# One attention and feed-forward kernel in another order, with its first weight loaded in 128-partition quarters

## The chip, the cores and the metric

The kernel runs on one core of a Trainium2 chip. Time is device time in microseconds (us) of one execution of the whole program; lower is better. Before the change three runs took 333.37, 333.5 and 333.9 us, median 333.5 us. The engines of the core have short names in the profile: PE is TensorE (matrix products), PEld its weight loads, DVE is VectorE, ACT is ScalarE, POOL is GpSimd and SP is SyncE. Each engine works through its own instructions strictly in order.

## The reference

Causal attention over 8 batches, 8 heads, 576 positions and 64 dimensions, with 16 "beacon" keys and values in front that every position may see, and then a two-layer feed-forward net with an ELU between its layers:

```
scores = q @ concat(beacon_k, k).T / sqrt(64), causal on the part of k
x = softmax(scores) @ concat(beacon_v, v)        -> 4608 tokens x 512
h = x @ w_in                                     -> 4608 x 2048
out = elu(h) @ w_out                             -> 4608 x 512, fp32
```

All inputs and the output are fp32 in DRAM; the kernel casts to 16 bits while loading.

## The kernel before

The program is one long list of small steps. `run(names)` at the end of the kernel takes words such as `F.4.6`, calls the step `F` with the arguments 4 and 6, and so issues its instructions to the engines' queues. Nothing reorders them: the place of a word in the list is its place in each queue that it uses, and waits on semaphores follow from the data and from the reuse of buffers. The words that matter here:

- `lq.b.n.h0.h1`, `lv.b.js`, `wi.c`, `wo.i`, `lk.b.n`: loads on POOL's DMA queue. `lq` brings q and k of a batch (0 to 2) straight into SBUF (L136); `lv` the values (L144, L149); `wi.c` a part of `w_in` (function `load_wi`, L161); `wo.i` a quarter of the rows of `w_out` (L165); `lk` copies q or k of a later batch (3 to 7) to a DRAM scratch in bf16 (L759). POOL's DMAs use eight semaphores in turn, so that each DMA is issued only when the eighth before it has landed.
- `lt.b.x`: two transposing DMAs from that scratch into SBUF, on SP's queue (L766), where the stores of the output stand too (`s`, L572, and those of `J`, L645).
- `T`, `cq`, `ck`, `cb`: for batches 0 to 2, transposes of q and k on PE (L265) and their copies out of PSUM (L278).
- `S.b.g`: a piece of 512 (batch 0: 416) columns of the scores of a batch on PE (L319); `x.b.g`: its exp on ACT (L334); `m`: the causal mask on DVE (L339). `S`, `L`, `W` and the `T` of batches 1 and 2 share two PSUM buffers of tag "S".
- `L`: sums of the exps on PE (L376, L418); `n`: their reciprocal, two ACT instructions (L433, L436); `W`: the product with the values on PE (L376); `M`: the scaled result into the feed-forward's input `xT` on DVE (L470 to L487). Parts `A` and `B` of batch 0 belong to tokens 0 to 255 and 256 to 575.
- `F.t.i`: 512 columns' worth of `h` for token tile t on PE (L510), into one of two PSUM buffers of tag "hps". Tiles 0 and 1 have 256 tokens, the other eight 512. `e` (exp, L520, ACT), `u` (relu, L526 on ACT or, with a `v` at the end, L528 on DVE) and `k` (L538, DVE) make the ELU from it. For the last two tiles part of `F` is done by a Strassen-like scheme: `X`, `H` (DVE), `P` (PE, L696), `K`, `E`, `U`, `V`.
- `G` (L559): the second product for tiles 0 and 1; `Q.t.a.b` (L626): for the others, in the Strassen-like form with `Z` and `wt` on DVE (L580) and `J` (L635 to L645) for what leaves PSUM. `o`, `s`: copy and store for tiles 0 and 1. `Jh` are the last two stores of the last tile.
- `warm` and `wm`: matmuls on zeros that keep PE busy while nothing has arrived. `tri`, `ident`: POOL makes the masks. `lp`: POOL pads keys of later batches (L775, L776).

`w_in` is held as 128 partitions x 4 (parts of the 512 rows) x 2048 columns in fp16. `load_wi(c)` has been called twice, for c = 0 and 1, each time with eight DMAs of 32 partitions x 2 parts x 1024 columns:

```
    def load_wi(c):
        f_ = slice(DF // 2 * c, DF // 2 * (c + 1))
        for g in range(2):
            for i in range(4):
                nc.gpsimd.dma_start(
                    out=w_in16[32 * i:32 * (i + 1), 2 * g:2 * g + 2, f_], in_=wi_v[i, :, g, :, f_])
```

`F.t.i` reads 128 columns of `w_in` per PSUM half for tiles of 512 tokens (i = 0 to 15) and 256 columns for tiles 0 and 1 (i = 0 to 7); it can start when the DMAs of those columns have landed.

## Time and profile before

| what | value |
|---|---|
| median of three runs | 333.5 us (333.37 to 333.9) |
| profiled execution: first to last instruction (span) | 331.3 us; the median lies 2.2 us above it |
| PE busy | 322.5 us, 97% of the span, 3576 matmuls |
| DVE busy | 291.8 us, 88% |
| ACT busy | 274.9 us, 83% |
| POOL busy | 88.3 us, 27% |
| granted TensorE clock | 0.998 of full speed |

A line of the timeline or of the chain has the start in us, the length in us, the engine, the source line, the operation and the tiles as output<-inputs, and at the end the idle time before it with what ended it. A line of a group has the number of instructions after an x, then the group's busy time in us and the mean length of one in ns. Instructions of one engine overlap a little, so a mean is longer than the step from one to the next. A line of waits has the total in us, the number of waits and the longest. A line of windows has the stretch, its length, and the busy time of PE, PEld, DVE, ACT and POOL with the instructions in brackets, then the clock, the DMA share and GB/s.

### The profile page before, as it was taken

Reading aid. Unit: us, or ns where it says so; the run is one execution under the profiler, and the core shown is the slowest. Engines: PE = TensorE matmul, PEld = TensorE weight load, DVE = VectorE, ACT = ScalarE, POOL = GpSimd, SP = SyncE. Lnnn points to the kernel's source line nnn. Section 1 sums busy time; section 2 is a strip of 40 time slices with the busy share of each in tenths; the row PEclk is TensorE's granted clock in tenths of the full one; section 3 lists DMA queues with packets and bytes.
Section 4 is the critical chain, followed back from the end, with each engine's and each line's share of the span. In section 5 each row is a group of like instructions: output and inputs, shape, how many; then the busy total and the mean of one; then the engine's idle time right before and its main releaser. Section 6 shows DMA issues by size and latency. Waiting matters only on the chain.

```text
span 331.3 us, 8764 instructions
## 1 busy us (share of the span) xinstructions
PE 322.5 (97%) x3576; PEld 208.3 (63%) x3576; DVE 291.8 (88%) x614; ACT 274.9 (83%) x446; POOL 88.3 (27%) x117
## 2 busy tenths in 40 slices
PE   8889999999999999999999999999999999999995
PEld 4657765544446565655665665556656788788784
DVE  3866888989998999999999789999999999999962
ACT  1898998699999998998898789996889687798730
POOL 8888266664008805000830050000000000000000
PEclk9999999999999999999999999999999999999999
DMA  9999999999989998952999098101100011011112
GB/s 114 172 169 182 199 191 172 160 148 156 164 193 69 172 164 135 97 117 60 104 192 153 3 110 133 33 0 34 66 32 3 33 65 34 32 65 34 64 66 95
DMA packets 129113, 34.66 MB, mean 105 GB/s; under 512 B 112944, under 2 KB 127536, under 8 KB 129072
## 3 DMA queue, kind: packets, MB, share of 16 engines
q0 software_dynamic: 94944, 18.49, 67.9%
q1 hardware_dynamic: 33408, 15.34, 20.8%
q8 instruction: 28, 0.46, 0.6%
q10 hardware_dynamic: 720, 0.26, 0.3%
q14 instruction: 13, 0.11, 0.1%
HBM read 37.22 MB, written 15.34 MB: 159 GB/s over the span
## 4 chain that ended last, share of the span: by engine, by line
PE 80%; DMA 10%; POOL 4%; ACT 2%; DVE 1%; issue 1%; DVEq 0%; POOLq 0%
PE hps L510 27%; PE ops L626 27%; DMA v<-in_v_dram 6%; PE sc L319 6%; PE ut L376 6%; PE hps L696 6%; PE ops L559 4%; DMA w_out<-in_moe_w_out_dram 3%; PE sx L626 2%; PE lt L376 1%; POOL qst L136 1%; POOL kst L136 1%; ACT et L334 1%; PE lt L418 1%; POOL v L149 1%
## 5 line engine op out<-in xcount | busy, mean ns | idle before, releaser
L510 PE MATMUL hps<-xT,w_in 128*128 128x512 f16 (+1 forms) x544 | 118.6, 355 | 0.3 <-DVE gt L550 0.2
L334 ACT ACTIVATE et<-sc 128x1024 f16<-128x1024 f32 (+2 forms) x114 | 103.6, 979 | 10.9 <-PE sc L319 10.8
L520 ACT ACTIVATE e<-hps 128x512 f32<-128x512 f32 x120 | 73.2, 617 | 18.9 <-PE hps L510 17.8
L626 PEld LDWEIGHTS <-gt 128*128 128x128 f16 x768 | 73.4, 98 | 19.9 <-issue 3.7
L538 DVE SCALAR_TENSOR_TENSOR gt<-e,r 128x512 f16<-128x512 f32 x112 | 75.4, 684 | 5.7 <-ACT r L526 5.0
L510 PEld LDWEIGHTS <-w_in 128*128 128x128 f16 x544 | 50.6, 98 | 41.9 <-issue 3.9
L526 ACT ACTIVATE r<-hps 128x512 f16<-128x512 f32 x88 | 54.3, 619 | 0.0
L626 PE MATMUL ops<-w_out,gt 128*128 128x256 f16 x368 | 48.0, 273 | 0.0
L626 PE MATMUL ops<-wt,gt 128*128 128x256 f16 x352 | 47.3, 273 | 0.0
L149 POOL DMA_DIRECT2D v<-in_v_dram x40 | 34.7, 914 | 10.6 <-DMA scr<-in_q_dram 3.6
L339 DVE TENSOR_TENSOR et<-et,triu 128x512 f16<-128x512 f16 (+4 forms) x108 | 31.6, 331 | 2.1 <-ACT et L334 2.1
L580 DVE TENSOR_TENSOR gt<-gt 128x1024 f16<-128x1024 f16 x48 | 32.2, 683 | 0.6 <-PE ops L626 0.3
L376 PEld LDWEIGHTS <-v 128*32 128x32 f16 (+1 forms) x800 | 17.4, 96 | 11.6 <-issue 4.2
L392 DVE TENSOR_TENSOR qk<-qk,et 128x672 f16<-128x672 f16 (+2 forms) x66 | 23.3, 367 | 0.5
L376 PE MATMUL ut<-et,v 128*32 128x464 f16 (+3 forms) x560 | 21.3, 296 | 0.0
L144 POOL DMA_DIRECT2D v<-in_beacon_v_dram x8 | 4.8, 595 | 61.8 <-PE lt L376 48.6
L528 DVE TENSOR_SCALAR r<-hps 128x512 f16<-128x512 f32 x24 | 16.4, 685 | 3.1 <-ACT e L520 2.8
L470 DVE TENSOR_TENSOR xT<-ut,rl 128x672 f16<-128x672 f32 (+12 forms) x26 | 16.4, 669 | 1.2 <-PE ut L376 0.7
L642 DVE TENSOR_TENSOR osb<-ops,sm 128x512 f32<-128x512 f32 x23 | 15.7, 682 | 1.0 <-PE ops L626 1.0
L559 PE MATMUL ops<-w_out,gt 128*128 128x512 f16 x64 | 16.4, 381 | 0.0
L735 DVE SCALAR_TENSOR_TENSOR gt<-e,r 128x512 f16<-128x512 f32 x24 | 15.9, 681 | 0.0
L706 ACT COPY kst<-hps 128x512 f32<-128x512 f32 x18 | 10.6, 588 | 5.9 <-PE hps L696 5.8
(113 smaller groups left out, 417.9 us busy)
## 6 DMA issues: line engine op xcount, KB each, us to landing
out_dram<-osb SPq DMA_DIRECT2D x35, 256.0 KB, 2.4
v<-in_v_dram POOLq DMA_DIRECT2D x24, 128.0 KB, 8.4
scr<-in_k_dram POOLq DMA_DIRECT2D x5, 576.0 KB, 12.8
scr<-in_q_dram POOLq DMA_DIRECT2D x5, 576.0 KB, 12.6
w_in<-in_moe_w_in_dram POOLq DMA_DIRECT2D x16, 128.0 KB, 5.5
w_out<-in_moe_w_out_dram POOLq DMA_DIRECT2D x4, 512.0 KB, 10.4
qst<-in_q_dram POOLq DMA_DIRECT2D x4, 288.0 KB, 9.4
kst<-in_k_dram POOLq DMA_DIRECT2D x4, 288.0 KB, 10.0
```

The lines of the kernel that those rows point to most:

```text
L149: nc.gpsimd.dma_start(out=vt[b][r0:r0 + n, j, :, :], in_=v[b, :, ilo[j]:ilo[j] + n, :].rearrange("h s d -> s h d"),)
L334: nc.scalar.activation(out=ets[b, d][:, :, a - EC2 * d:e - EC2 * d], in_=sc[b, g][:, :, a - c0:e - c0], func=AFT.Exp, bias=0.0, scale=SCALE)
L339: nc.vector.tensor_tensor(out=o, in0=o, in1=i, op=ALU.mult)
L376: nc.tensor.matmul(out=t[32 * i:32 * (i + 1), a - qa:e - qa], lhsT=ones[0:kc[j], :] if half is None else v16[0:kc[j], j, h, 32 * half:32 * ...
L392: (nc.vector if eng == "v" else nc.gpsimd).tensor_tensor(out=o, in0=t[0:rows, :, a:e] if n == 0 else o, in1=t[0:rows, :, col:col + e - a], ...
L510: nc.tensor.matmul(out=h[:, n_, :], lhsT=w_in16[:, cc, P * fc:P * (fc + 1)], rhs=xt[k][:, cc, a - TT * k:e - TT * k], start=(cc == 0), sto ...
L520: nc.scalar.activation(out=eb[t, i], in_=flat(hp[t, i]), func=AFT.Exp, bias=0.0, scale=1.0)
L526: nc.scalar.activation(out=rb[t, i], in_=flat(hp[t, i]), func=AFT.Relu, bias=0.0, scale=1.0)
L538: nc.vector.scalar_tensor_tensor(out=half(t, i), in0=eb[t, i], scalar=1.0, in1=rb[t, i], op0=ALU.subtract, op1=ALU.min)
L559: nc.tensor.matmul(out=ob[t, tb_], lhsT=gt[:, fc, P * tb_:P * (tb_ + 1)], rhs=w_out16[:, fc, :], start=(fc == 0), stop=(fc == NFC - 1))
L580: (nc.vector if eng == "v" else nc.gpsimd).tensor_tensor(out=o_, in0=a_, in1=b_, op=op_)
L626: nc.tensor.matmul(out=xy[t, n_][:, qd, :], lhsT=lw[:, P * qd:P * (qd + 1)], rhs=wt_[:, c, :], start=(first and c == 0 and (qd == 0 or (t, ...
```

## The change

Two functions and the list differ.

```diff
-    wi_v = moe_w_in.rearrange("(g i t d) f -> i d g t f", i=4, t=2, d=32)
+    wi_v = moe_w_in.rearrange("(g i t d) f -> g t i d f", i=4, t=2, d=32)
...
     def load_wi(c):
-        f_ = slice(DF // 2 * c, DF // 2 * (c + 1))
-        for g in range(2):
-            for i in range(4):
-                nc.gpsimd.dma_start(
-                    out=w_in16[32 * i:32 * (i + 1), 2 * g:2 * g + 2, f_], in_=wi_v[i, :, g, :, f_])
+        f_ = slice(DF // 4 * c, DF // 4 * (c + 1))
+        for cc in range(NCC):
+            nc.gpsimd.dma_start(out=w_in16[:, cc, f_], in_=wi_v[cc // 2, cc % 2, :, :, f_])
...
     def P_(t, g, ph):
-        if ph == 0:
+        if (t, g, 0) not in hx:
```

`w_in` still comes in 16 DMAs with the same bytes each, but a DMA now fills 128 partitions of one part and 512 columns, and `wi.0` to `wi.3` are four steps of four DMAs, one for each quarter of the columns, that stand apart in the list. The test in `P_` lets its phases come in another order.

The list has the same words as before, except that `wi.0` and `wi.1` have become `wi.0` to `wi.3`; all 1503 others are there once each, most of them at another place. The start and the places that the prediction names:

```diff
-    warm.4 lq.0.0.0.4 warm.4 lq.0.1.0.4 warm.4 wm.4 ident wm.4 T.0.0.0 bt wm.4 bk wm.4 wm.4
-    T.0.1.0 cb.0.0 cq.0.0.0 S.0.0.0 x.0.0.0 T.0.1.1 lq.0.0.4.8 cq.0.1.0 cb.0.1 S.0.1.0 x.0.1.0
...
-    M.0.A.1 x.1.2 S.1.1 x.1.1 W.0.A.0 M.0.A.0 S.0.3.3 x.0.3.3 S.0.2.2 wi.0 F.0.2 x.0.2.2 S.1.5
...
-    x.2.3 L.1.0 n.1.0 wt.1.0 G.0.1.2 H.1.2 M.1.0.0 W.1.0 u.1.0.v M.1.0.1 L.1.1 k.1.0 e.0.7 F.1.6
-    m.2.0.0 n.1.1 M.1.1.0 cb.2.3 W.1.1 M.1.1.1 e.1.6 u.0.7 u.1.6.v k.1.6 S.2.2 x.2.2 G.0.0.2
...
-    Q.9.77.84 Q.9.84.91 J.9.4 Q.9.91.98 J.9.5 Q.9.98.105 Jh.9.0 Q.9.105.112 Jh.9.1
+    warm.4 warm.4 wm.4 wm.4 wm.4 lq.0.0.0.4 lq.0.1.0.4 ident T.0.1.0 lq.0.0.4.8 bt cq.0.1.0 bk
+    warm.4 T.0.0.0 cb.0.1 cb.0.0 cq.0.0.0 S.0.1.0 T.0.1.1 S.0.0.0 x.0.1.0 x.0.0.0 T.0.0.1
...
+    x.0.0.2 m.0.0.2 S.0.2.3 x.0.2.3 L.0.A lv.0.0.1 n.0.A T.1.0.0 wi.0 T.1.1.0 W.0.A.1 cq.1.0.0
+    wm.4 lv.0.3.4 m.0.2.3 ck.1.1.0 S.0.3.2 x.0.3.2 M.0.A.1 W.0.A.0 wi.1 S.0.3.3 m.0.2.2 M.0.A.0
+    x.0.3.3 S.0.2.1 F.0.1 cb.1.2 S.0.3.1 cb.1.3 m.0.0.3 m.0.3.2 x.0.2.1 m.0.3.3 e.0.1 lq.1.0.4.8
+    S.1.4 x.0.3.1 wo.0 x.1.4 m.0.1.2 H.1.0 F.0.0 e.0.0 u.0.0 L.0.B W.0.B.1 k.0.0 wi.3 n.0.B
+    u.0.1.v F.0.2 e.0.2 u.0.2 M.0.B.1 W.0.B.0 M.0.B.0 S.1.3 x.1.3 F.0.3 S.1.5 e.0.3 k.0.1
...
+    e.1.4 m.1.0.1 H.2.2 ck.2.0.0 k.0.7 m.1.1.0 u.1.4.v x.2.4 L.1.1 L.1.0 lp.3.1 n.1.1 F.1.6
+    cb.2.0 M.1.1.0 k.1.4 n.1.0 M.1.0.0 lv.1.2.3.4 W.1.1 wo.2 W.1.0 M.1.1.1 S.2.7 wo.3 lk.3.1
...
+    k.2.14 x.3.1 Z.2.3.0 wt.4.0 k.2.3 Q.2.0.7 s.1.1 F.3.3 o.1.0 x.3.12 e.3.3 D.3.1.1 S.3.2
...
+    Q.2.14.21 D.3.1.2 Z.2.1.1 lk.4.0 lt.4.0 S.4.2 S.4.1 x.4.1 Q.2.21.28 k.3.3 D.3.1.3 J.2.0
...
+    F.4.10 e.4.10 u.4.10 e.4.14 Q.3.42.49 J.3.2 x.5.7 Q.3.56.63 F.4.6 F.4.12 D.4.3.3 u.4.6 e.4.6
...
+    Q.9.63.70 Z.9.4.0 Q.9.70.77 J.9.3 Q.9.77.84 Q.9.84.91 J.9.4 Q.9.91.98 J.9.5 Q.9.98.105 J.8.6
+    Q.9.105.112 Jh.9.0 Jh.9.1
```

## The prediction

> **What bounds the kernel now.** I read the first part of the page, then the stretches, then the groups of ACT, the waits, the chain and single places of the timeline.

> ```profile
> span 331.3 us, 8764 instructions
> PE 322.5 (97%) x3576; PEld 208.3 (63%) x3576; DVE 291.8 (88%) x614; ACT 274.9 (83%) x446; POOL 88.3 (27%) x117
> PE 80%; DMA 10%; POOL 4%; ACT 2%; DVE 1%; issue 1%; DVEq 0%; POOLq 0%
> 8.80:60.20 51.40, 48.58 (x906) 33.30 (x909) 40.15 (x95) 46.48 (x65) 35.40 (x51) 1.00 1.53 180
> 60.20:150.85 90.65, 90.65 (x899) 48.83 (x892) 85.27 (x182) 83.67 (x133) 31.27 (x34) 1.00 1.59 144
> 9.20:151.25 142.05, 139.23 (x1797) 82.17 (x1796) 125.42 (x276) 130.56 (x197) 66.28 (x83) 1.00 1.57 157
> 151.25:331.30 180.05, 175.66 (x1724) 122.20 (x1721) 162.94 (x329) 143.09 (x249) 14.13 (x17) 1.00 0.36 62
> ```

> PE is the bound: from 60.20 to 150.85 it is busy in 90.65 of 90.65 us, and it heads the chain with 80%. Since the change adds no matmul, the time can only grow by new holes in PE's work and shrink by filling old ones, which lie in the first 60 us and at the end. But ACT is close behind, with 130.56 of 142.05 us (91.9%) from its first exp to 151.25. The new list moves work between engines' queues, so the second engine is what I count.

> **The change, part by part.** *The loads.*

> ```profile
> L161 POOL DMA_DIRECT2D w_in<-in_moe_w_in_dram x8: 532/535/571, 13.1 to 19.5; - x8
> L165 POOL DMA_DIRECT2D w_out<-in_moe_w_out_dram x2: 762/764/765, 28.7 to 29.4; - x2
> 12.26 6.96 DMA v<-in_v_dram
> 29.40 10.87 DMA w_out<-in_moe_w_out_dram
> 23.89 0.69 DVE L480 TENSOR_TENSOR xT<-ua,rl 128x512 f16<-128x512 f32 x1 [0.32 <-PE ua L376]
> 24.70 1.05 PE L510 MATMUL hps<-xT,w_in 128*128 128x256 f16 x8
> ```

> Sixteen DMAs of 128 KB stay. One takes POOL 0.535 us to issue; the nearest 128-partition form is the `w_out` row's 0.764, so the new ones cost POOL between 0 and 16 × 0.23 = 3.7 us more. I take 0: the chain shows POOL waiting for landings (6.96 and 10.87 us), which covers it; without that cover `wi.3` would be issued up to 3.7 us late, against the 4 to 9 us by which, in my walk through the new list, loads land ahead of their first reader. How fast they land is bounded by rows too: the values before them land at 12.26 + 6.96 = 19.22, the last of the old eight at 24.37 (issued 19.5, landing row below), 0.64 us per 128 KB; `w_out` in 128 partitions landed 512 KB in 37.3 to 40.3, 2.9 us or 0.73 per 128 KB. So a quarter is there at 19.22 + 4 × 0.64 = 21.8 to 19.22 + 4 × 0.73 = 22.1. I take 21.8, the price of the same DMA size.

> ```profile
> DMA to landing us min/median/max: 4.9/5.6/6.4
> DMA to landing us min/median/max: 8.7/9.8/10.9
> ```

> Before, the first `F` at 24.70 had two conditions 0.2 us apart: the weights at 24.37 and `xT`, finished at 23.89 + 0.69 = 24.58. After, `F.0.1` stands behind `M.0.A.0`, and my walk has it near 22.5, about 2 us earlier.

> *The first stage.* That lead isn't kept. (The walk takes the new list word by word, each word's instructions at the lengths that the trace before has for them, each waiting for the words that it reads and for the buffers that it takes.) In it `F.0.2` waits about 1.3 us for a PSUM bank of tag hps, because `u.0.1.v` stands on DVE behind `k.0.0`; and `L.1.1 L.1.0 W.1.1 W.1.0` hold both S buffers, so that after `x.2.4` no scores can be made and ACT stands some 1.6 us. The end of `W.1.0` comes out at 60.2, and PE's matmuls behind it sum to what was left before at 60.20 too. So the start is worth 0 here (bounds: −2.2, the lead kept, and +2).

> *The stage to `F.4.6`.* At the word `F.4.6` PE has the same work left as before at 150.85, so that place measures the gain. `F.4.6` needs the bank that `u.4.10` frees, and behind ACT's part of that stand these in the list: 81 exps of scores, 57 exps and 38 relus of `F`, 18 instructions of reciprocals, 4 copies of keys, 3 of `J`. Before, up to 151.25:

> ```profile
> L334 ACT ACTIVATE et<-sc 128x1024 f16<-128x1024 f32 (+2 forms) x77 | 69.2, 974 | 9.2 <-PE sc L319 9.2
> L520 ACT ACTIVATE e<-hps 128x512 f32<-128x512 f32 x59 | 36.3, 621 | 6.3 <-PE hps L510 5.5 <-ACT sm L635 0.5 <-ACT hi L278 0.2
> L526 ACT ACTIVATE r<-hps 128x512 f16<-128x512 f32 x37 | 23.0, 624 | 0.0
> L436 ACT ACTIVATE rl<-rl 128x576 f32<-128x576 f32 (+2 forms) x8 | 5.5, 684 | 0.3
> L433 ACT ACTIVATE rl<-lt 128x576 f32<-128x576 f32 (+1 forms) x7 | 4.9, 693 | 1.9 <-PE lt L376 1.9
> L278 ACT COPY qk<-tp 128x1152 bf16<-128x1152 bf16 x3 | 3.3, 1112 | 0.8 <-PE tp L265 0.8
> L635 ACT COPY sm<-ops 128x512 f32<-128x512 f32 x4 | 2.4, 591 | 0.1
> L278 ACT COPY hi<-tp 128x1152 bf16<-128x1152 bf16 x1 | 1.2, 1180 | 0.0
> L433 ACT ACTIVATE rl<-la 128x512 f32<-128x512 f32 x1 | 0.7, 695 | 0.0
> L334 ACT ACTIVATE et<-sc 128x1024 f16<-128x1024 f32 x84 | 84.2, 1052 | 3.2 <-PE sc L319 3.1
> 9.20 1.62 ACT L334 ACTIVATE et<-sc 128x832 f16<-128x832 f32 x2 [7.12 <-PE sc L319]
> ```

> (The last but one is the full-size exps of the whole run.) The difference is 4 exps of scores more, 2 of `F` fewer, a relu and 2 reciprocal instructions more, a `J` copy fewer: +4 × 1.052 − 2 × 0.621 + 0.624 + 2 × 0.684 − 0.591 = +4.4 us. ACT's instructions overlap: these groups of the stretch (the first nine rows) sum to 146.5 us where 130.56 are busy, a factor of 0.89, so +3.9. ACT thus has 130.6 + 3.9 = 134.5 us to do by `F.4.6`, from about 8.8 on (before from 9.20). When it gets through depends on how densely it works, and the rows give 91.9% (whole stretch), 95.7% and 97.6%:

> ```profile
> 140.00:160.00 20.00, 20.00 (x238) 11.72 (x236) 19.10 (x44) 19.14 (x31) 1.04 (x2) 1.00 0.36 75
> 20.00:30.00 10.00, 9.28 (x218) 6.67 (x215) 5.67 (x15) 9.76 (x14) 8.57 (x15) 1.00 1.17 166
> ```

> By 91.9% `F.4.6` comes at 8.8 + 134.5 / 0.919 = 155.2; by 95.7% at 149.3; by 97.6% at 146.6. I take two stages. Up to 60.2 ACT did 46.48 us before. Ahead of `W.1.0` the new list has 31 exps of scores against 33, 14 of `F` against 15 and 6 relus against 5:

> ```profile
> L334 ACT ACTIVATE et<-sc 128x832 f16<-128x832 f32 (+2 forms) x33 | 28.2, 941 | 7.7 <-PE sc L319 7.7
> L520 ACT ACTIVATE e<-hps 128x512 f32<-128x512 f32 x15 | 9.1, 609 | 1.5 <-PE hps L510 1.2 <-ACT hi L278 0.2
> L526 ACT ACTIVATE r<-hps 128x512 f16<-128x512 f32 x5 | 3.0, 607 | 0.0
> ```

> That is −2 × 0.941 − 0.609 + 0.607 = −1.9, of which I let 0.7 be filled by words from behind (bounds 0 and 1.9): 45.3, or 88%. The remaining 134.5 − 45.3 = 89.2 I put at 95.7%, the value where ACT and PE both ran full, since ACT now is what PE waits for: 93.2 us. `F.4.6` then starts at 60.2 + 93.2 = 153.4, 2.55 us later than 150.85. That is 93.0% over all. The density at which nothing changes is 134.5 / (150.85 − 8.8) = 94.7%, or 94.4% with the tail below.

> Behind `F.4.6` ACT has 3.9 us less to do than before in 180.05 us with 143.09 busy, and PE with 175.66 busy bounds again; I count 0 there (±1).

> *The store queue.* SP works in order. The new list puts `lt.4.0` (the transposes of batch 4's keys and queries) directly behind `s.1.1`, a store that waits for `o.1.1` near 94, and `S.4.2` needs them at 100 to 103. The two prices of a transpose from issue to landing:

> ```profile
> L766 SPq DMA_TRANSPOSE kst<-scr x2: 2630/3445/4260, 70.0 to 72.7; - x2
> DMA to landing us min/median/max: 8.7/9.5/11.4
> L766 SPq DMA_TRANSPOSE kst<-scr x2: 1291/1612/1934, 87.0 to 91.5; - x2
> DMA to landing us min/median/max: 3.3/3.8/5.5
> ```

> (First pair from 60 to 83 us, while POOL's queue was full; second from 86 to 100, while it was quieter.) Landing lies between 94 + 3.3 = 97 (no stall) and about 94 + 11.4 = 105 (up to 5 us of PE). I take the quiet price, as the stretch is the nearest, hence 0 in the sum; the other end is a rival. `s.0.0` and `s.1.0`, moved later, hold two of three output buffers while `J.2.4` to `J.2.6` need them; stores land in 2.4 us against about 3.5 between `J`s, so 0 (bounds 0 to 3).

> ```profile
> out_dram<-osb SPq DMA_DIRECT2D x35, 256.0 KB, 2.4
> ```

> *The tail.* PE's last product waits for the copy of `Jh.9.0`:

> ```profile
> 326.34 0.37 ACT L746 COPY osb<-sx 128x256 f32<-128x256 f32 x1 [3.89 <-PE sx L626]
> 326.76 0.92 PE L626 MATMUL sx<-wt,gt 128*128 128x256 f16 x7 [0.46 <-ACT osb L746]
> ```

> With `Q.9.105.112` ahead of `Jh.9.0` that 0.46 goes: −0.5 (bounds −0.5 and 0, if `J.8.6`, now between, takes its place). `tri`, one place later on POOL, and `P`'s test cost nothing: POOL there waits for landings, and the test runs on the host.

> *The sum.* The profiled execution took 331.3 us of span and about 2.2 around it, equal to the 333.5 us median: 333.5 + 0 (start) + 2.55 (`F.4.6` later) + 0 (store queue) − 0.5 (tail) = 335.5.

> [...] The row: the old 32-partition loads landed at 0.64 us per 128 KB and the 128-partition `w_out` at 0.73. [...]

> **The rivals.**

> *The other side: ACT stays dense.* The new order feeds ACT so that it works at 95.7% from its first exp on, not only behind 60 us. For it: 97.6% between 20 and 30 us in the old list, where weights had just come. Against it: the exps of the first 60 us waited 7.7 us for scores (row above). `F.4.6` at 149.3, −1.55, and −0.5: 331.4. It ends faster from 94.4% on. At 97.6% it would be 333.5 − 4.25 − 0.5 = 328.8, the lowest I can construct.

> *Late transposes.* `lt.4.0` at the busy price: PE stands at `S.4.2`, ACT has no scores of batch 4 either, +3 (middle of 0 to 5 rounded up) on top of the forecast: 338.5, at most 340.5. For it: POOL's queue still carries `lk.4.0` just ahead of it. Against it: before, the transposes at 87 to 96 were quick.

> *The start was held by the load.* A quarter in place of a half is what matters, and the 2.6 us from 24.70 to 22.1 are kept through the first stage, ACT keeping pace: 333.5 + 2.55 − 2.6 − 0.5 = 332.9. For it: the first `F` follows the last landing by 0.3 us. Against it: `xT` was 0.12 us ahead of that `F`, so the load alone gave nothing.

> *Nothing changes.* The later `F.4.6` is only PE work in another order, PE finds filler, and the holes add to what the tail gives: 333.5.

> **How the numbers follow.** Forecast 0.38; late transposes 0.18; dense ACT 0.24; the load 0.10; nothing 0.10. The forecast is 335.5, its own range 334.2 (94.0% dense) to 337.5 (91.9%, rounded down for the part past 60 us). 0.2%, 0.67 us, is about what a measurement here can tell. Faster: dense ACT 0.24 and the load at 332.9 mostly, 0.08, with 0.02 of "nothing": 0.34. Same: 0.10, from "nothing" and the lower edge of the forecast. Slower: the rest, 0.56. The range goes from 328.8, the lowest of dense ACT, to 340.5, the highest of late transposes.

> **What would show it.** In the trace after: first `F` near 22.5, its weights landed by 22.1; the end of `W.1.0` near 60.2; ACT 88% busy up to there and near 95% from there; `F.4.6` near 153.4, with PE's waits there put down to relus or exps of ACT; `lt.4.0` landed before `S.4.2`; no wait of PE for `osb` in the last 2 us. Wrong would make me: an end of `W.1.0` more than 1 us from 60.2 (the first stage), PE standing for `kst` near 100 us (the queue), or a PE that stays without holes to 150 (ACT not bounding).

## The result, and the profile after

The changed kernel takes 346.7 us (median of four runs, 345.2 to 350.8) against 333.7: a ratio of 1.036, 95% interval 1.031 to 1.042. That is 12 to 13 us slower and above the 340.5 us at which my range ended. A ratio, here and below, leaves out a run that is more than 1.5% above the fastest of its kernel (here the one of 350.84 us). The profiled execution took 345.23 us, with a span of 343.5.

The first parts of the page of the kernel after (the rows of PE, PEclk and DMA show, in 40 slices of 8.6 us, the busy share of PE, the granted clock and the busy share of the DMA engines, in tenths), and its stretches, with the last two rows for the kernel before:

```profile
span 343.5 us, 8750 instructions
PE 325.3 (95%) x3576; PEld 209.8 (61%) x3576; DVE 290.5 (85%) x614; ACT 276.6 (81%) x446; POOL 92.3 (27%) x117
PE   6979999995999999889999999999999999999995
PEclk9998999999899999989999999999999999999999
DMA  9999999999999441999597090610110011020113
PE 79%; DMA 9%; ACT 4%; POOL 3%; DVE 2%; issue 2%; SPq 1%; DVEq 0%; POOLq 0%
```

```profile
8.80:60.20 51.40, 48.77 (x916) 33.48 (x916) 37.81 (x95) 46.31 (x65) 37.73 (x54) 0.97 1.47 168
60.20:150.85 90.65, 81.76 (x806) 42.37 (x798) 75.92 (x158) 75.78 (x116) 36.80 (x35) 0.97 1.59 137
164.35:343.50 179.15, 175.07 (x1684) 122.81 (x1681) 161.59 (x325) 140.33 (x244) 10.14 (x14) 1.00 0.29 58
8.80:164.35 155.55, 144.03 (x1859) 84.05 (x1855) 125.84 (x280) 135.03 (x202) 74.53 (x88) 0.97 1.54 149
8.80:150.85 142.05, 139.23 (x1799) 82.14 (x1800) 125.42 (x276) 130.16 (x197) 66.67 (x83) 1.00 1.57 157
150.85:331.30 180.45, 176.06 (x1728) 122.56 (x1725) 163.34 (x329) 143.49 (x250) 14.13 (x17) 1.00 0.36 63
```

Where PE had no hole before, from 60.20 to 150.85, it now lacks 8.9 us of 90.65, and the clock of this stretch is 0.97. `F.4.6` begins at 164.35, 13.5 us later than the 150.85 of before, and PE has about the same work left there (175.07 us busy against 176.06). Behind it the new order is 1.3 us quicker (179.15 us against 180.45), most of it this 1.0 us. So the loss is complete by `F.4.6`. The rows from 8.80 us to `F.4.6` divide it: PE was idle there for 155.55 − 144.03 = 11.5 us against 2.8 before, 8.7 more, and busy for 144.03 us against 139.23, 4.8 more; together 13.5. The idle part first. The longest waits of PE behind the first 8.8 us, and where they stand in its timeline:

```profile
PE sc L317 <- DMA qst<-scr: 4.2, 2, 3.5
PE hps L508 <- DVE r L526: 3.1, 1, 3.1
PE sc L317 <- issue: 2.1, 2, 1.9
PE sc L317 <- DMA kst<-scr: 1.4, 1, 1.4
```

```profile
23.66 0.38 PE L317 MATMUL sc<-hi 64*128 64x80 bf16 x5 [1.86 <-issue]
23.98 1.05 PE L508 MATMUL hps<-xT,w_in 128*128 128x256 f16 x8
...
78.87 0.39 PE L317 MATMUL sc<-kst 64*128 64x272 bf16 x4 [1.38 <-DMA kst<-scr]
...
86.46 0.40 PE L317 MATMUL sc<-qst 64*128 64x48 bf16 x6 [3.47 <-DMA qst<-scr]
...
109.71 0.63 PE L317 MATMUL sc<-qst 64*128 64x16 bf16 x10 [0.73 <-DMA qst<-scr]
...
147.54 1.20 PE L508 MATMUL hps<-xT,w_in 128*128 128x512 f16 x4 [3.09 <-DVE r L526]
```

There are five holes of over 0.3 us, 10.5 us together. None of them is put down to ACT. In order: `S.0.3.3`, which waits for nothing that the profile names; `S.3.8` and `S.3.3`, for the transposes of batch 3; `S.4.2`, for those of batch 4; and `F.4.1`, for a relu on DVE.

The busy part is the clock. Stretches after three of these holes, in the windows of the kernel after:

```profile
26.00:27.00 1.00, 1.00 (x7) 0.64 (x6) 0.96 (x6) 1.00 (x3) 0.51 (x1) 0.50 0.94 74
88.50:90.00 1.50, 1.50 (x5) 0.42 (x3) 0.15 (x1) 1.08 (x2) 0.93 (x1) 0.50 2.47 158
150.00:152.00 2.00, 2.00 (x14) 0.97 (x13) 2.00 (x5) 1.18 (x2) 0.00 (x0) 0.58 1.89 215
```

By the clock records of the trace the grant falls to 0.50 three times, for 3.4 us each, at 25.4, 86.8 and 148.3 us, 0.3 to 1.7 us behind the end of the holes of 1.86, 3.47 and 3.09 us. Each costs half of 3.4, so some 1.7 us, 5.1 in all, in which PE counts as busy. That is an estimate, and it roughly fits the 4.8 us by which PE was busy longer.

The last hole has its cause on DVE and SP:

```profile
146.20 0.69 DVE L638 COPY osb<-ops 128x512 f32<-128x512 f32 x1 [3.52 <-DMA out_dram<-osb]
```

`J.2.6` (L638) waits for an output buffer. `o.0.0` and `o.1.0` have filled two of the three and their stores stand far behind in the new list, so `J.2.4`, `J.2.5` and `J.2.6` share one; the store of `J.2.5` was issued at 139.73 and landed at 146.11. `u.4.9.v`, next on DVE, is what `F.4.1` needs.

### The profile page after: what moved, and what is told of

It is laid out like the page before. It is cut to its first block, busy times and chain, and to the rows that moved or that the text cites. A ratio compares the mean times of both kernels' runs of the same rounds, so it can differ in the third digit from the quotient of the medians.

```text
span 343.5 us, 8750 instructions
## 1 busy us (share of the span) xinstructions
PE 325.3 (95%) x3576; PEld 209.8 (61%) x3576; DVE 290.5 (85%) x614; ACT 276.6 (81%) x446; POOL 92.3 (27%) x117
## 4 chain that ended last, share of the span: by engine, by line
PE 79%; DMA 9%; ACT 4%; POOL 3%; DVE 2%; issue 2%; SPq 1%; DVEq 0%; POOLq 0%
PE hps L508 27%; PE ops L624 24%; PE sc L317 7%; PE hps L694 5%; PE ut L374 5%; DMA qst<-scr 5%; PE ops L557 4%; DMA v<-in_v_dram 2%; PE sx L624 2%; DMA out_dram<-osb 2%; PE lt L374 2%; ACT et L332 1%; PE tp L263 1%; POOL qst L136 1%; POOL kst L136 1%
## 5 line engine op out<-in xcount | busy, mean ns | idle before, releaser
L332 ACT ACTIVATE et<-sc 128x1024 f16<-128x1024 f32 (+2 forms) x114 | 104.6, 967 | 23.6 <-PE sc L317 23.5
L508 PE MATMUL hps<-xT,w_in 128*128 128x512 f16 (+1 forms) x544 | 120.4, 359 | 3.1 <-DVE r L526 3.1
L624 PEld LDWEIGHTS <-gt 128*128 128x128 f16 x768 | 74.6, 98 | 19.3 <-issue 2.0
L518 ACT ACTIVATE e<-hps 128x512 f32<-128x512 f32 x120 | 71.8, 613 | 10.1 <-PE hps L508 9.8
L524 ACT ACTIVATE r<-hps 128x512 f16<-128x512 f32 x88 | 52.7, 611 | 5.4 <-PE hps L508 4.5
L624 PE MATMUL ops<-w_out,gt 128*128 128x256 f16 x368 | 49.1, 277 | 0.0
L624 PE MATMUL ops<-wt,gt 128*128 128x256 f16 x352 | 46.5, 273 | 0.0
L149 POOL DMA_DIRECT2D v<-in_v_dram x40 | 35.6, 1036 | 6.8 <-issue 4.4
L526 DVE TENSOR_SCALAR r<-hps 128x512 f16<-128x512 f32 x24 | 16.4, 685 | 11.1 <-ACT e L518 11.1
L144 POOL DMA_DIRECT2D v<-in_beacon_v_dram x8 | 5.9, 738 | 43.1 <-PE lt L374 22.1
L317 PE MATMUL sc<-qst 64*128 64x80 bf16 (+13 forms) x160 | 12.4, 258 | 4.2 <-DMA qst<-scr 4.2
## 6 DMA issues: line engine op xcount, KB each, us to landing
out_dram<-osb SPq DMA_DIRECT2D x35, 256.0 KB, 2.4
```

What stands on the lines that cost most here:

```text
L149: nc.gpsimd.dma_start(out=vt[b][r0:r0 + n, j, :, :], in_=v[b, :, ilo[j]:ilo[j] + n, :].rearrange("h s d -> s h d"),)
L317: nc.tensor.matmul(out=s[:, h, a - c0:e - c0], lhsT=t[D * h:D * (h + 1), 1, P * j:P * (j + 1)], rhs=t[D * h:D * (h + 1), 0, NB + qa + a - ...
L332: nc.scalar.activation(out=ets[b, d][:, :, a - EC2 * d:e - EC2 * d], in_=sc[b, g][:, :, a - c0:e - c0], func=AFT.Exp, bias=0.0, scale=SCALE)
L508: nc.tensor.matmul(out=h[:, n_, :], lhsT=w_in16[:, cc, P * fc:P * (fc + 1)], rhs=xt[k][:, cc, a - TT * k:e - TT * k], start=(cc == 0), sto ...
L518: nc.scalar.activation(out=eb[t, i], in_=flat(hp[t, i]), func=AFT.Exp, bias=0.0, scale=1.0)
L524: nc.scalar.activation(out=rb[t, i], in_=flat(hp[t, i]), func=AFT.Relu, bias=0.0, scale=1.0)
```

## The experiments

Theories that the runs tell apart: **L**, the shape of the loads makes the DMA queue slower, so that everything behind is late; **O**, the new order does it by itself, by its queues (held buffers, transposes) or, as I had forecast, by asking too much of ACT; **F**, the hole near 22 us is a late instruction fetch.

**The loads alone, in the order before.**

```diff
-wi.0 F.0.2 ...   wi.1 F.0.4        (8 loads each: 32 partitions x 2 parts x 1024 columns)
+wi.0 wi.1 F.0.2 ...   wi.2 wi.3 F.0.4        (load_wi as after)
```

> The order before, with only w_in loaded in the new way (each half as two quarters, at the old places). Theory L (the load shape): a quarter load in 128 partitions makes 128 packets of 1024 B and some 384 of 4 B where the old one makes 64 of 2048 B, which in the traces is 283 us of DMA engine time for all of w_in against 190, or +5.8 us on 16 saturated engines. What is behind it on POOL's queue lands about 3.6 us later, and with it the scratch of batch 3 and its transposes, which batch 3's first scores need: PE stands 1 to 4 us near 82, with half clock behind it, 336 to 339 us. Theory O (the order alone is at fault): 333.7 us, no hole.

338.3 us against 334.5, ratio 1.012 (1.008 to 1.017). Theory O alone is out, as this order is the one of before; L's size came out, but not its place. The holes, in PE's timeline of this kernel:

```profile
37.62 0.45 PE L263 MATMUL tp<-identb,qst 96*64 96x96 bf16 x12 [1.83 <-DMA qst<-in_q_dram]
39.39 0.45 PE L263 MATMUL tp<-identb,kst 96*64 96x96 bf16 x12 [1.32 <-DMA kst<-in_k_dram]
```

It is not batch 3's transposes but the direct loads `lq.1.0.4.8` of batch 1, the next behind `w_in` on POOL's queue, that come late. Windows of the same kernel (its 20 to 30 and 30 to 40 us) beside the second of the kernel before, whose first stands in the prediction with 166 GB/s:

```profile
20.00:30.00 10.00, 8.74 (x184) 5.95 (x182) 4.98 (x14) 9.11 (x13) 7.62 (x11) 1.00 1.27 134
30.00:40.00 10.00, 6.85 (x160) 4.92 (x146) 6.32 (x12) 6.43 (x11) 6.13 (x10) 0.99 1.21 174
```

```profile
30.00:40.00 10.00, 9.88 (x173) 7.18 (x162) 8.99 (x16) 8.61 (x14) 4.97 (x8) 1.00 1.24 195
```

The queue moves 134 and 174 GB/s where it moved 166 and 195, with its engines as busy (the DMA share is 1.27 and 1.21 against 1.17 and 1.24). By the packet records the old loads are 1024 packets of 2048 B at 185 ns; the new ones are 1024 B at 106 ns, twice as many, and 6144 packets of 4 B besides.

**The old loads in the order after** (halves, at the places of `wi.0` and `wi.3`).

> The order after, with w_in loaded in the old way (32 partitions, halves, at the places of the first and the second quarter to be called). Theory L: the lag of the queue goes, batch 3's transposes land 3 to 4 us earlier, so of the holes 1.38 and 3.47 us and the half clock behind them (1.7 us) 4 to 5.5 us go; the hole of 1.86 us near 22 may go too, if it is a late instruction fetch in a full queue: 338 to 343 us. Theory O: 346 us, holes as they are.

345.0 us (341.6 to 346.3), ratio 1.031 (1.025 to 1.037). Four holes of over 2 us are there; the waits of PE:

```profile
PE sc L319 <- DMA qst<-scr: 5.0, 2, 2.6
PE hps L510 <- DVE r L528: 3.1, 1, 3.1
PE hps L510 <- DMA w_in<-in_moe_w_in_dram: 2.1, 1, 2.1
```

Batch 3's holes fall from 4.85 to 2.4 us, but batch 4's grows from 0.73 to 2.6: PE came to `S.4.2` 4.4 us earlier (at 104.6 in place of 109.0), and the transpose that it reads landed only 2.5 us earlier (107.2 in place of 109.7). A first half of `w_in` that lands later than the first quarter did takes another 2.1. So L explains only a part, and a hole that is taken away shows the next. The time itself is not clearly below the changed kernel's: the two intervals, 1.025 to 1.037 and 1.031 to 1.042, overlap. The span and mean clock of this execution have a second lesson, that with four holes of 2.1 to 3.2 us the clock stayed whole:

```profile
core 0: 339.9 us, clock 0.997
```

**The stores early, in the order after.**

```diff
-... F.6.4 s.0.0 D.6.2.2      ... k.4.9 s.1.0 Q.3.14.21
+o.0.0 s.0.0 M.2.0.0 ...      lt.4.1 s.1.0 F.3.12
```

> The order after, with the stores s.0.0 and s.1.0 put where their data is ready (behind o.0.0 and behind lt.4.1), so that only one of the three output buffers is in use for long. If the 3.09 us hole near 144 comes from the two held buffers, it goes, and with it the half clock behind it (1.6 us): 341.5 to 342.5 us. If it comes from a slow store alone, a hole of 1 us or more stays: 344 to 346 us.

344.1 us, ratio 1.031 (1.027 to 1.036). The hole near 144 is gone altogether, so the held buffers were its cause. Of the 4.7 us expected 2.6 came, by medians whose intervals overlap: at `S.4.2` there is now the wait

```profile
112.37 0.63 PE L317 MATMUL sc<-qst 64*128 64x16 bf16 x10 [2.86 <-DMA qst<-scr]
```

**The loads in 128 partitions, but in halves of 1024 columns.**

> The order after, w_in in 128 partitions but 1024 columns to a load (8 loads, two halves). By packet size (Theory L): 1024 packets of 2048 B as in the old loads and half as many of 4 B, some +2 us of queue in place of +5.8: the transposes of batch 3 come 2 to 3 us earlier than after the change, 340 to 344 us. If the span of partitions and not the packets sets the landing (32 partitions slower or faster than 128), it differs from the old loads in the new order by more than 2 us.

345.5 us, ratio 1.030 (1.025 to 1.036), no different from the old loads in this order. By the rule of the expectation that speaks against the span of partitions, but in this order the time doesn't tell the forms of the load apart (346.7, 345.0 and 345.5 us); the packet records do. The packets are of 2048 B again, and yet, in the packet records, they take 249 ns each in place of 185. By 40 us the queue has moved 5.66 MB, against 5.58 after, 6.07 with the old loads in this order and 6.29 before. So the packet's size isn't what costs: by the packet records a load that spans 128 partitions with one part of the rows costs more than the old form with either size of packet. Why, no run here shows.

**Batch 4's transposes ahead of the store**, on top of the early stores.

```diff
-Q.2.0.7 s.1.1 ... lk.4.0 lt.4.0 S.4.2
+Q.2.0.7 lk.4.0 lt.4.0 s.1.1 ... S.4.2
```

> As the run with early stores, and the transposes lt.4.0 put ahead of s.1.1 on SP's queue (lk.4.0 keeps its place on POOL's queue). If lt.4.0 was late because it stood behind a store that waited for DVE, it is issued near 93 instead of 102 and the hole at S.4.2 (2.86 us in the run with early stores, 0.73 in the new order itself) goes, with or without a half clock behind it: 339.5 to 341.5 us. If the transfers themselves are late, the hole stays: 344 us.

339.8 us, ratio 1.018 (1.014 to 1.022): 4.3 us less than the run before it, and no hole of PE over 0.25 us is left behind 88 us. The transfers are no quicker (issue to landing 9.9 us in the median between 85 and 115 us, against 5.4 in the run with early stores), only begun 8.5 us sooner: first issued at 94.2 in place of 102.7.

```profile
L764 SPq DMA_TRANSPOSE qst<-scr x4: 1235/2596/5745, 94.2 to 112.4; - x4
DMA to landing us min/median/max: 7.6/9.9/11.1
```

**Batch 3's first users later**, on top of that.

```diff
-D.2.1.3 S.3.8 x.3.8 e.2.11 F.2.7 L.2.0 ... W.2.0 F.2.9 S.3.3 F.2.8 ... G.1.0.0 x.3.3
+D.2.1.3 e.2.11 F.2.7 L.2.0 ... W.2.0 S.3.8 x.3.8 F.2.9 F.2.8 ... G.1.0.0 S.3.3 x.3.3
```

> As the last, and S.3.8 and S.3.3, the first users of batch 3's transposes, put 3 and 2 us of PE work later in the list. If the holes at 77 to 87 are there because the list asks for batch 3 earlier than its scratch is through (need 77.5 against a landing at 78.8 and 86.4), most of the 3.7 to 4.9 us goes, with the half clock behind: 335 to 338 us. If ACT is what bounds this stage (my forecast's theory, a density of 93%), PE waits for ACT instead and no more than 1 us is won.

340.7 us, ratio 1.020 (1.016 to 1.025): nothing won. The first hole went into the second:

```profile
79.83 0.39 PE L317 MATMUL sc<-kst 64*128 64x272 bf16 x4 [0.57 <-DVE xT L468]
...
87.26 0.82 PE L317 MATMUL sc<-qst 64*128 64x48 bf16 x10 [4.34 <-DMA qst<-scr]
```

`S.3.3` starts at the landing: at 86.5 in the kernel after, 88.7, 87.8 and 87.3 in the last three of its order and loads (early stores, batch 4, batch 3). The chain that sets it is steady: from the landing of batch 3's second scratch (`lk.3.0`) to the last of its four transposes go 18.5 to 19.3 us, 67.1 to 86.4 after, 68.6 to 87.7 and 68.3 to 87.2 in the last two runs, and 63.6 to 82.5 before. What moves it is when the scratch lands, and that has a spread of its own: 67.1 to 69.3 us in the four traces with the new loads whose lists are the same up to there (after, early stores, batch 4, batch 3).

**The old loads**, on top of that (`load_wi` and the two places as above).

> As the last, with the old loads of w_in. All four causes that I see are undone but the order itself: if they are all there is, PE runs full from 31 us on and the time is that of before or a little under, 331.5 to 334.5 us, still with a hole of some 2 us near 23 us, where the half of w_in lands later than a quarter. If the new order has a cost of its own (ACT's density), 335 us or more.

335.2 us (ten runs, 333.4 to 336.8), ratio 1.003 (1.001 to 1.006): 5.5 us less than the run before it, which is what the loads cost in this mended list. The scratch lands at 64.5, the last transpose at 83.1. With the four causes undone, the order after is within 0.6% of before.

**The fillers.** Four traces (after; wide halves; batch 3 later; with old loads) have the hole near 22 us at the same matmul, in the middle of `S.0.3.3`, with "issue" as its releaser. To test F, each `wm.4` became one matmul about as long as its four (in the trace after the 48 matmuls of the twelve `wm.4` take 4.2 us, the 12 of 512 columns of the `warm.4` 4.6):

```diff
-wm.4        (12 times, four matmuls and four weight loads of 128 columns)
+warm.1      (one matmul of 512 columns)
```

> The order after with one edit: each of the twelve fillers wm.4 (four matmuls of 128 columns on zeros) is one matmul of 512 columns, the same PE time with 6 fewer instructions on PE's queue, 72 in all. In four traces PE stands at the very same place, before its 705th recorded instruction, in the middle of S.0.3.3 and with nothing to wait for. Theory F (a late instruction fetch, once for every 256 instructions): the place belongs to the count, so the hole leaves S.0.3.3; the 256 instructions up to the next fetch then take longer than the 4 us that they take now, and no hole of over 1 us put down to issue is left by 30 us: 1.9 us less, with the half clock 3.5 us less, 343 to 345 us. Theory W (a wait of S.0.3.3 that the profile doesn't name): the hole stays at S.0.3.3, 346 us.

The hole left `S.0.3.3`, and one came at another word:

```profile
31.75 1.03 PE L508 MATMUL hps<-xT,w_in 128*128 128x256 f16 x8 [1.20 <-issue]
```

Counted in PE's records (its sequencer's included), the gaps of over 0.6 us put down to issue stand at these places:

```
kernel                          before record   us from the record before to it
after                           705             2.05
wide halves                     705             3.14
batch 3 later                   705             1.94
with old loads                  705, 1985       1.77, 0.87
old loads, order after          961             0.90
after, wide fillers             961             1.28
all and wide fillers            1729            1.00
all but S.3.8                   1729            0.62
```

705, 961, 1729 and 1985 lie 256 or a multiple of 256 apart, whatever word stands there. The profile's queue of instructions has 28 transfers in 0.46 MB, of 16 KB each, and PE has 7178 records, 256 to a transfer. So theory F holds: PE ran through 256 instructions, from record 450 at 17.7 us to 705 at 21.6, before the next 16 KB, fetched between other packets at 21.2, were there. At all nine places of the table PE goes on 1.3 to 1.8 us behind the end of such a packet (at 23.66 behind 22.16 in the trace after). The time didn't gain by it: 349.5 us, ratio 1.045 (1.041 to 1.049), expected 343 to 345. The profiled execution had 14.0 us of holes and a granted clock of 0.971, three stretches at half of 6.8 us each. Of the 2 us at the start 0.9 us were left at `S.3.8`, where PE came at 76.6 in place of 77.5, and its transpose landed at 80.2 in place of 78.8, so PE waited 3.65 us there; for batch 4 it waited 3.95 us, 1.1 us earlier at a transpose that was 2.1 us later. Why they landed later, no run shows; the scratch of batch 3 came at 68.6, within the spread given above.

**All of it with wide fillers; the same with `S.3.8` back at its place; and the order before with wide fillers.**

> The order after with early stores, batch 4's transposes ahead of s.1.1, batch 3's first users later, the old loads, and the wide fillers. Theory F: the hole of 1.57 us at S.0.3.3 goes, and the two half-clock windows behind it in the profile; the wait for w_in near 24 (0.78 us) stays or grows to 2: 331.5 to 334 us against 335.2. Theory W: 335 us.

> As the run with all and the wide fillers, with S.3.8 and its exp back at their place, since with the old loads its transposes are there in time and the two S buffers had to wait for exps where it was moved to (0.57 + 0.90 + 0.32 us of holes at 81 to 89): 1 to 1.5 us less than that run, 330.5 to 333 us. If ACT's density were the cost of the new order, as I forecast, it would be no faster than 335 us.

> The order before with the wide fillers alone. It has no hole of this kind, so by theory F nothing is to be won or lost unless the shifted count puts a dense stretch into one fetch: 333 to 335 us, as before.

335.3 us (1.006; 1.003 to 1.009), 335.0 us (1.004; 1.002 to 1.007) and 334.3 us (1.003; 1.000 to 1.006). None beats the kernel before, the first two miss what was expected of them, and neither step moved the time measurably from 335.2. The hole of the fetch near 22 us is gone in the first two, and the place that it freed is taken by the half of `w_in`:

```profile
24.80 0.81 PE L510 MATMUL hps<-xT,w_in 128*128 128x256 f16 x6 [2.25 <-DMA w_in<-in_moe_w_in_dram]
```

That line is from the run with `S.3.8` back, and so is this row, which settles the question of ACT:

```profile
90.00:150.00 60.00, 59.98 (x648) 34.75 (x646) 58.15 (x123) 57.94 (x92) 22.94 (x23) 1.00 1.57 140
```

PE is busy in 59.98 of 60 us while ACT works at 96.6%. `F.4.6` is at 154.5, 3.7 us after the 150.85 of before; the holes and one stretch at half clock that lie ahead of it make it so. The likely rest against before is that hole for `w_in` and the half clock behind it; that it is was not tested.

**The tail, in the order before** (`Q.9.105.112` ahead of `Jh.9.0`).

> The order before, with Q.9.105.112 ahead of Jh.9.0, the one place of the tail that I gave a gain: PE's wait of 0.46 us for the copy of Jh.9.0 goes. By my step 0.5 us less, 333.0 to 333.4 us; if the last store sets the end and not PE, no change.

The hole of 0.46 us is gone from the trace; the time is 333.8 us, ratio 0.9995 (0.997 to 1.002). A gain of 0.5 us (0.15%) can neither be shown nor excluded by twelve runs.

## Why the prediction was wrong

The sign was right and the reasons, for the most part, were not: 335.5 forecast, 340.5 the top of the range, 346.7 measured. In the terms of the sum: the 2.55 us for ACT brought no wait of PE; the store queue, put at 0, cost 3.8 us of holes; the late transposes of batch 3, which have no term, 4.85; a late fetch of instructions, which has none either, 1.86; and the half clock behind the holes some 5.1. That the forecast had the sign right is luck, since the term that gave it brought nothing.

- **ACT (the forecast's 2.55 us).** Wrong, though the count was right: by `F.4.6` ACT had done 135.03 us of work, forecast 134.5. PE's five holes have other causes, and with these undone ACT ran at 96.6% from 90 to 150 us under a full PE. All that PE waited for ACT in that execution is 1.5 us for exps, near 84 to 88, and 0.2 for a relu, no more than the 1.7 us of before. I had derived a wait from a count of work without a hole in the trace to carry it. That `F.4.6` stands at 154.5 there, close to the forecast 153.4, is therefore a coincidence.
- **The store queue, "hence 0 in the sum".** This step failed. For the held buffers I set 2.4 us for a store (the median of the whole run) against 3.5 us between the `J`s; the store in question took 6.4, in a stretch in which POOL's queue moved 0.87 MB beside it, and PE stood 3.09 us, a little over my upper bound, with half a clock behind it. For `lt.4.0` I took the quiet price of 3.8 us; it is one of 5 to 10 us and begun at 102. It cost 0.73 us in the trace after and 2.6 to 4.0 in four other traces with its place unchanged, where PE came earlier or the transpose landed later. The rival of the late transposes named this mechanism, with +3 and a chance of 0.18; the mechanism was there, but it is only one part of the loss.
- **Batch 3's transposes (4.85 us, the largest part of the holes)** stand in no step, which is the term that was missing. The new list asks for them at 77.5 us and before it landed them at 82.5. I should have set the need of each transfer against its landing one by one, as I did with `lt.4.0`.
- **The loads.** "I take 21.8" for the first quarter; it landed at 22.5, 0.4 us past my bound. What I didn't see is that the price falls on everything behind: by 40 us the queue has moved 0.5 MB less than with the old loads in the same order (5.58 against 6.07). I had bounded POOL's time for the issues and the landing of the first quarter, and left the rate for all that follows as it was. By the run of the loads alone it costs 3.8 us in the order before, and 5.5 in the mended order after.
- **32 or 128 partitions.** The two rows, 0.64 us per 128 KB against 0.73, pointed the right way: the first quarter landed at 22.5, and with wide halves a 2048 B packet of a 128-partition load took 249 ns against 185 ns of a 32-partition one. The rival in which the load gains falls: the loads cost time in either order (ratio 1.012 in the order before, 5.5 us in the mended order after).
- **The start, 0.** Right by the sum and wrong by its terms. `W.1.0` ends at 61.2, 1 us past my 60.2, although the fetch and the half clock behind it took 3.5 us: a lead of some 2.5 us was there, and PE's instruction supply took it, which my walk doesn't know. In the run with wide fillers, without that hole, the time was no shorter.
- **The rival "nothing changes"** falls with the measured ratio. **The dense ACT**, the other side, has its density only in part: 86.8% from 8.80 us to `F.4.6` in the trace after (135.03 of 155.55 us), and 96.6% from 90 to 150 us with the causes undone. It had no price for holes, so its time was as far off.
- **The tail.** The trace agrees (no wait for `osb` at the end, and behind `F.4.6` 1.3 us less); it is too small to be measured.
- **A slip in the sums:** a density of 94.0%, the lower end of the forecast's own range, gives 334.0 and not 334.2. Nothing hangs on it.

Two things made the sum so short. I priced each wait at its quiet value and by itself, where all of them fall into stretches with full DMA engines (the row DMA is 9 up to 112 us and again from 138 to 163). And I had no term for the clock, which added half as much again to the holes.

## What to carry to other kernels

Where the DMA engines are full, set for each transfer the time at which the new order needs it against its landing in the trace, and take landings from the same stretch, not a median of the run; a moved store also holds its buffer, so count how many are left. A hole that is taken away can be paid back at the next late transfer: here the four steps brought 2.6, 4.3, 0 and 5.5 us, and only together the way back. And in these traces a hole in PE could cost more than its length, from about half of a 3.4 us step on (the clock fell behind 4 of 8 steps with 1.57 to 1.82 us of idle time and behind all 14 with 2.05 or more): 1.7 us on top, or twice that.

## What the runs showed of the hardware

```
PE idle in the step of 3.41 us     steps     half clock in the next
0.90 to 1.51 us                    18        2 (both behind a step of about 2.5 us or more)
1.57 to 1.82 us                     8        4
2.05 to 3.37 us                    14        14
```

So in these traces what counts is idle time in one step, at about half of it, and a hole of 3.15 us that is cut in two by the grid (1.64 and 1.51, old loads in the order after) passes. Four falls lie outside the table: three prolong a half clock behind a step with 0.62 to 0.83 us of idle time, and one, in the order before with wide fillers at 14.4 us, comes at a full clock behind 0.82 us and is not explained. Where the grid lies against the program differs from trace to trace: counted in steps of 61.44/18 us from the start of the span, it is off by 1.5 us after, by 0.9 with the wide fillers, and by 2.6 before (from the fall at its end, at 330.3). That this is a reason why runs of one kernel spread is likely, not tested: the order after had clocks of 0.970 to 0.984 and 345 to 351 us, the order before 0.994 to 1.000 and 332 to 336.

PE's instructions came in blocks of 256 (28 transfers of 16 KB for 7178 records), and a dense stretch of short matmuls (255 records in 3.9 us) outran the fetch while the DMA engines were full (the row DMA is 9 there in the trace after): in four traces the next record came 1.8 to 3.1 us after the one before it.
